# A two-layer mixer on one core: transfers of the divided sixth product moved from layer 1 to layer 0, and low parts used last

## The chip, the cores and the metric

One core of one Trainium2 chip. The metric is device time of one execution, in microseconds (us); runs of the same kernel differ by some tenths of a per cent. The work is matmuls in fp32 accuracy on TensorE (PE), with VectorE (DVE), ScalarE (ACT) and GpSimd (POOL) preparing operands, and two engines' queues issuing DMAs: SP (SyncE) and POOL.

## What is computed

The reference runs a linear-attention block and a gMLP block, twice, on x of 2048 x 512:

```python
def _A_ref(x, wqkv, wo):               # 32 heads of 16
    q, k, v = ...                      # x @ wqkv, split in heads
    pq, pk = phi(q), phi(k)            # phi(t) = (t + 1 if t > 0 else exp(t)) + 1e-6
    kv = einsum("bhsd,bhse->bhde", pk, v)
    z = einsum("bhsd->bhd", pk)
    o = (pq @ kv) / (pq . z + 1e-6)
    return o @ wo
def _B_ref(x, w_in, w_sp, b_sp, w_out):
    z = gelu(x @ w_in)                 # 2048 x 1792
    z1, z2 = z[..., :896], layernorm(z[..., 896:])
    g = w_sp @ z2 + b_sp               # w_sp is 2048 x 2048
    return (z1 * g) @ w_out
x = x + _A_ref(layernorm(x)); x = x + _B_ref(layernorm(x))   # layer 0
x = x + _A_ref(layernorm(x)); x = x + _B_ref(layernorm(x))   # layer 1, same weights
```

## The kernel before

**Stages.** Each layer (L = 0, 1) has four: P1 (class `P1`: K, Q, phi and the 512 x 512 product of k and v, a step s per 128 rows of x), P2 (the attention's output, then x @ w_in, gelu and layernorm, again by 128-row tiles, with a `tail` in layer 1), P4 (class `P4`: w_sp @ z2, the spatial mixing) and `out7` (the output stage, z1 * g times w_out, eight steps j, x added by accumulating DMA stores of POOL).

**Three matmuls for one.** Every fp32 operand is split in a high part (fp32r, made by ACT: L1678 for w_sp, L214 elsewhere) and a low part (operand less high part, made by DVE: L1681 for w_sp, L217 elsewhere). Each product runs as high x high, high x low, low x high (`mm3`, L228 to L230; for the spatial mixing `acc`, L1889 to L1891; in the output stage L2087 to L2089; in the tail L1145 to L1147).

**The spatial mixing.** w_sp @ z2 is cut into 2 x 2 blocks and done with seven block products instead of eight (a Strassen-Winograd scheme), in the order P2, P1, P6, P7, P4, P5, P3. A product is eight steps k, one per 128 rows of its block; in a step PE takes about 4.07 us. A product in `DIVIDED` (P2 and P4 in layer 0; P2, P4 and P5 in layer 1) is itself done by seven products of half the size, 7 x 2 steps (`SEVEN` gives their order; `mm_div`). The sixth product, P5, is so divided in layer 1 alone: this is the divided sixth product of the title.

**Sums of w_sp.** The products need sums of blocks of w_sp. Class `Sums` holds them in DRAM scratch, since both layers use the same w_sp: `s` and `s1` (made in layer 0's first half), `halves` (tile names hP: quarter sums that the divided products need) and `lows` (lowP). A hP tile of P4 or P5 is made in two transfers by `halve`: a *copy* from DRAM to DRAM on SP (L1551), 512 KB, and later an *add*, an accumulating DMA of POOL (L1555), 512 KB. `Sums.parts` lists them: 0 to 7 copies and 8 to 15 adds for P4, 16 to 23 copies and 24 to 31 adds for P5. `PARTS` says at which step of layer 0's mixing a part of P4 is issued; `P1.run` issues those of P5 in layer 1's steps s = 2 to 17 by `sums.halve(14 + s, None)`.

**Kept low parts.** `kept` names steps of P7 and P5 whose low part of w_sp layer 0 stores (SP, L1686) and layer 1 loads (POOL, L1684) in place of the subtraction L1681. With P5 divided in layer 1, six of its fourteen steps (k = 0, 1, 6, 7, 12, 13) take a kept one.

**What sets the order.** The schedule is written by hand: each engine executes in the order of the program, and so do SP's and POOL's DMA queues. `fetch1` (L1657, L1662) issues raw halves of w_sp on SP, `wsp` splits them two steps ahead of PE, `zsp` splits z (L1743 is the low part of z), `gate` (L1928 on DVE, L1930 on POOL) multiplies a finished unit of g by a page of z1, loaded on SP (L196, pg<-z). `wraw` loads pages of w_out on SP (L196, pg<-in_wout_dram). In layer 1's tail `wfetch` issues loads of sums of w_in on POOL (L205, pg<-w1s and pg<-w), and `e3` makes the layernorm's mean and variance of two z2 tiles with small column operations of POOL (L1074 in `e3m`; L1086 to L1088).

## Time and profile before

| what | value |
|---|---|
| median of 3 runs | 1353.8 us (1351.34 to 1356.03) |
| the profiled execution | 1351.78 us, its span 1350.0 us |
| TensorE clock granted | 1.00 |
| DMA | 294.50 MB, mean 218 GB/s |

In the profile a line of a group says the source line, the engine, the operation and `out<-in` by tile names: pg, qd and bg are pages (128 x 512), quads and larger tiles in SBUF, bank a PSUM bank, hP and lowP the scratch above. A row of a timeline is start, duration, engine, line, operation, and in brackets the idle time before it with what ended it. A row of windows gives the stretch, its length, busy time and number of instructions of PE, its weight loads, DVE, ACT and POOL, then the granted clock, the share of the sixteen DMA engines and GB/s. A row of DMA issues gives the size of one and the median us from issue to landing. A row of waits gives the total, the number and the longest.

From about 350 to 614 us runs the mixing of layer 0, to 692 its output stage, to 806 layer 1's P1, to 1016 its P2 with the tail, to 1272 its mixing (P7 from 1130, P5 from 1201) and to 1346 its output stage.

### The profile page before, as it was taken

The numbers are of one execution on the slowest core, as the hardware profiler recorded it, in microseconds if no ns is written. First come the engines' busy times: TensorE is split into PE (matmuls) and PEld (weight loads), VectorE is DVE, ScalarE is ACT, GpSimd is POOL, SyncE is SP. The second block draws the span as 40 slices with busy tenths as digits, with TensorE's granted clock in tenths as the row PEclk, the third lists the DMA queues.
The fourth block names the chain that finished last, engine by engine and source line by source line (L and its number), as shares of the span: only waits on it lengthen the run. The fifth ranks groups of instructions, "written<-read, shape, count | busy, mean of one in ns | idle before, by whom it ended". The sixth has DMA issues, their size and how long they took to land.

```text
span 1350.0 us, 19217 instructions
## 1 busy us (share of the span) xinstructions
PE 1340.0 (99%) x6540; PEld 1141.3 (85%) x6540; DVE 1037.7 (77%) x1658; ACT 726.3 (54%) x1219; POOL 463.8 (34%) x613
## 2 busy tenths in 40 slices
PE   9999999999999999999999999999999999999998
PEld 7888888888888888889988888888888888877898
DVE  7679877763797689897866877777689757889885
ACT  5774544334643255445667755556687333656454
POOL 3765765544122300301435453545450023022021
PEclk9999999999999999999999999999999999999999
DMA  5898477878877996843678783678767447479343
GB/s 183 277 311 281 164 264 252 289 262 263 296 241 266 299 292 208 291 164 64 152 192 287 208 199 94 204 249 252 235 195 252 143 171 264 155 242 315 106 78 64
DMA packets 174515, 294.50 MB, mean 218 GB/s; under 512 B 14544, under 2 KB 53968, under 8 KB 174160
## 3 DMA queue, kind: packets, MB, share of 16 engines
q1 hardware_dynamic: 155280, 253.67, 55.9%
q0 software_dynamic: 19136, 39.59, 13.4%
q8 instruction: 51, 0.84, 0.2%
q14 instruction: 48, 0.39, 0.1%
HBM read 206.18 MB, written 103.81 MB: 230 GB/s over the span
## 4 chain that ended last, share of the span: by engine, by line
PE 86%; DVE 4%; DMA 4%; issue 3%; ACT 1%; POOL 1%; SPq 0%; DVEq 0%; POOLq 0%; ACTq 0%
PE bank L1890 12%; PE bank L1891 12%; PE bank L1889 12%; PE bank L230 11%; PE bank L228 11%; PE bank L229 11%; PE bank L2087 3%; PE bank L2088 3%; PE bank L2089 3%; DMA qd<-lowP 1%; PE bank L988 1%; PE bank L987 1%; PE bank L986 1%; DMA pg<-xt 1%; PE bank L2101 1%
## 5 line engine op out<-in xcount | busy, mean ns | idle before, releaser
L1890 PE MATMUL bank<-qd,pg 128*128 128x512 f32 x760 | 296.1, 390 | 2.5 <-DMA qd<-lowP 1.7
L1889 PE MATMUL bank<-qd,pg 128*128 128x512 f32 x760 | 295.7, 389 | 0.0
L1891 PE MATMUL bank<-qd,pg 128*128 128x512 f32 x760 | 295.7, 389 | 0.0
L1678 ACT ACTIVATE qd<-qd 128x1024 fp32r<-128x1024 f32 x142 | 149.6, 1054 | 143.0 <-PE bank L1891 115.5
L1681 DVE TENSOR_TENSOR qd<-qd,qd 128x1024 fp32r<-128x1024 f32 x128 | 162.1, 1268 | 60.4 <-ACT qd L1678 60.4
L230 PE MATMUL bank<-qd,pg 128*128 128x512 f32 x448 | 174.8, 390 | 0.0
L1890 PEld LDWEIGHTS bank<-qd,pg 128*128 128x128 f32 x760 | 142.7, 188 | 33.3 <-DMA qd<-lowP 2.8
L1889 PEld LDWEIGHTS bank<-qd,pg 128*128 128x128 f32 x760 | 142.7, 188 | 29.7 <-ACT qd L1678 0.2
L1891 PEld LDWEIGHTS bank<-qd,pg 128*128 128x128 f32 x760 | 142.7, 188 | 29.5
L1930 POOL TENSOR_TENSOR bg<-bg,pg 128x512 f32<-128x512 f32 x28 | 47.9, 1710 | 213.6 <-DVE bg L1944 99.6
L228 PE MATMUL bank<-qd,pg 128*128 128x512 f32 x308 | 120.3, 391 | 0.3 <-DVE pg L217 0.3
L229 PE MATMUL bank<-qd,pg 128*128 128x512 f32 x308 | 120.0, 390 | 0.0
L230 PEld LDWEIGHTS bank<-qd,pg 128*128 128x128 f32 x448 | 84.1, 188 | 18.6 <-DVE pg L217 1.0
L363 POOL TENSOR_SCALAR rs<-mv 128x1 f32<-128x1 f32 x80 | 24.6, 308 | 197.4 <-DVE mv L361 188.0
L372 ACT ACTIVATE pg<-pg,nb,rs 128x512 f32<-128x512 f32 x52 | 42.1, 812 | 85.0 <-POOL nb L366 78.6
L1587 POOL TENSOR_TENSOR pg<-pg,pg 128x512 f32<-128x512 f32 x48 | 67.4, 1403 | 58.4 <-DMA pg<-in_wsp_dram 56.5
L214 ACT ACTIVATE pg<-pg 128x512 fp32r<-128x512 f32 x85 | 53.0, 624 | 63.1 <-DVE pg L448 18.2
L2089 PE MATMUL bank<-wo,qd 128*128 128x256 f32 x288 | 81.4, 283 | 0.0
L2087 PE MATMUL bank<-wo,qd 128*128 128x256 f32 x276 | 78.1, 283 | 0.0
L2088 PE MATMUL bank<-wo,qd 128*128 128x256 f32 x276 | 78.0, 283 | 0.0
L228 PEld LDWEIGHTS bank<-qd,pg 128*128 128x128 f32 x308 | 57.8, 188 | 12.6 <-DVE pg L217 0.7
L229 PEld LDWEIGHTS bank<-qd,pg 128*128 128x128 f32 x308 | 57.8, 188 | 12.1 <-DVE qd L217 0.3
(270 smaller groups left out, 3242.2 us busy)
## 6 DMA issues: line engine op xcount, KB each, us to landing
qd<-s SPq DMA_DIRECT2D x62, 512.0 KB, 4.3
qd<-in_wsp_dram SPq DMA_DIRECT2D x40, 512.0 KB, 4.0
qd<-hP SPq DMA_DIRECT2D x40, 512.0 KB, 4.6
pg<-z SPq DMA_DIRECT2D x56, 256.0 KB, 3.9
pg<-in_wsp_dram SPq DMA_DIRECT2D x52, 256.0 KB, 4.3
s<-pg SPq DMA_DIRECT2D x48, 256.0 KB, 3.7
z<-pg SPq DMA_DIRECT2D x40, 256.0 KB, 3.1
pg<-w POOLq DMA_DIRECT2D x38, 256.0 KB, 4.6
```

The source lines that it names most:

```text
L228: nc.tensor.matmul(out, ah, bh, start=start, stop=False)
L229: nc.tensor.matmul(out, ah, bl, start=False, stop=False)
L230: nc.tensor.matmul(out, al, bh, start=False, stop=stop)
L1587: nc.gpsimd.tensor_tensor(t, a, b, op=OP.add)
L1678: self.mark = nc.scalar.activation(w[:, 0], r, AF.Copy)
L1681: nc.vector.tensor_sub(w[:, 1], r, w[:, 0].bitcast(F32))
L1889: m(out, h[:, o], w[:, 0, j, :], start=start, stop=False, skip_group_check=True)
L1890: m(out, h[:, o], w[:, 1, j, :], start=False, stop=False, skip_group_check=True)
L1891: m(out, l[:, o], w[:, 0, j, :], start=False, stop=stop, skip_group_check=True)
L2087: m(out, A, x, start=start and f == 0, stop=False, skip_group_check=True)
L2088: m(out, A, y, start=False, stop=False, skip_group_check=True)
L2089: m(out, B, x, start=False, stop=stop and f == 2, skip_group_check=True)
```

## The change

1. The eight copies of P5 move from layer 1's P1 (s = 2 to 9) to the steps k = 0 to 7 of layer 0's P3, by `PARTS`.
2. The adds 24 to 27 move from layer 1's P1 (s = 10 to 13) to the first four steps of layer 0's output stage, after `join_b`. The adds 28 to 31 are issued as two halves each (256 KB), at s = 9 to 16 of layer 1's P1 (they were at s = 14 to 17).
3. `kept` leaves out the first four steps of P7: layer 0 makes four lowP stores less, layer 1 four lowP loads less and four subtractions more.
4. In layer 1, the kept steps of P5 use the low part of w_sp after the eight matmuls of a step that use its high part.
5. In layer 1's tail the column operations of the last tiles are issued behind the loads of `wfetch`: two `e3m` behind the first, and the three `e3r` operations of two tiles behind the second.

The lines of the changed kernel are some 8 to 31 higher: L1555 becomes L1572, L1551 L1565, L1681 L1698, L1686 L1703, L1728 to L1743 L1745 to L1760, L1086 to L1088 L1094 to L1096, L1074 L1075, L1657 and L1662 L1674 and L1679.

In layer 0's P3, SP issued these transfers before (qd<-s: raw halves; pg<-z: pages of z1; pg<-in_wout_dram: w_out):

```order
L196 DMA pg_571_5774<-z_0_0_5_2576 128x512
L1662 DMA qd_19_3764<-s_6_143 128x1024
L196 DMA pg_574_5817<-z_0_0_6_2692 128x512
L196 DMA pg_575_5819<-in_wout_dram 128x512
L196 DMA pg_576_5821<-in_wout_dram 128x512
L1662 DMA qd_19_3764<-s_7_144 128x1024
L196 DMA pg_579_5850<-z_0_1_4_3090 128x512
L196 DMA pg_584_5884<-z_0_1_5_3107 128x512
L196 DMA pg_587_5926<-z_0_1_6_3223 128x512
L196 DMA pg_588_5928<-in_wout_dram 128x512
```

and issues now, from the second copy on:

```order
L1565 DMA hP_1_1_168<-s_145 16x8192
L196 DMA pg_574_5815<-z_0_0_6_2692 128x512
L196 DMA pg_575_5817<-in_wout_dram 128x512
L196 DMA pg_576_5819<-in_wout_dram 128x512
L1679 DMA qd_19_3764<-s_7_144 128x1024
L1565 DMA hP_3_0_166<-s_145 16x8192
L196 DMA pg_579_5849<-z_0_1_4_3090 128x512
L1565 DMA hP_3_1_170<-s_145 16x8192
L196 DMA pg_584_5884<-z_0_1_5_3107 128x512
L1565 DMA hP_2_0_165<-s_145 16x8192
L196 DMA pg_587_5927<-z_0_1_6_3223 128x512
L196 DMA pg_588_5929<-in_wout_dram 128x512
```

Two copies stand ahead of the page z_0_1_4 and four ahead of the third w_out page; four more copies follow between later pages of z1.

In layer 1's tail, POOL had this order before (acc: the columns of mean and variance; w1s, w_3 and on: sums of w_in for PE):

```order
L1086 TENSOR_SCALAR acc<-acc 128x1
L1087 TENSOR_TENSOR acc<-acc,mhalf 128x1
L1088 TENSOR_SCALAR acc<-acc 128x1
...
L1074 TENSOR_SCALAR acc<-acc 128x1 x2
L205 DMA pg_981_10265<-w1s_1_0_119 128x512
L205 DMA pg_982_10267<-w1s_1_1_120 128x512
L205 DMA pg_984_10303<-w_3_0_101 128x256
```

and has now:

```order
L205 DMA pg_981_10257<-w1s_1_0_119 128x512
L205 DMA pg_982_10259<-w1s_1_1_120 128x512
L205 DMA pg_984_10295<-w_3_0_101 128x256
L205 DMA pg_985_10297<-w_3_1_102 128x256
L1075 TENSOR_SCALAR acc<-acc 128x1 x2
L205 DMA pg_986_10310<-w_4_0_103 128x256
L205 DMA pg_987_10312<-w_4_1_104 128x256
L1094 TENSOR_SCALAR acc<-acc 128x1
L1095 TENSOR_TENSOR acc<-acc,mhalf 128x1
L1096 TENSOR_SCALAR acc<-acc 128x1
```

The column operations (three each for two tiles) have gone behind the loads w1s, w_3 and w_4, ahead of w_5.

At the start of layer 1's P7, DVE had the evacuation of the product before (L1947) and then the z work of one step after another; before:

```order
L1947 TENSOR_TENSOR bg_26_10485<-bank_360_10816,pg_980_10250 128x512
L1728 TENSOR_TENSOR pg_1074_11325<-z_z_8642 128x384
L1730 TENSOR_TENSOR z_z_8642<-z_z_8642,z_z_9514 128x384
L1732 TENSOR_TENSOR z_z_9514<-z_z_8642,z_z_9514 128x384
L1733 TENSOR_TENSOR z_z_9514<-z_z_9514,z_z_8642 128x128
L1743 TENSOR_TENSOR pg_1076_11331<-pg_1074_11325,pg_1075_11330 128x384
L1728 TENSOR_TENSOR pg_1078_11341<-z_z_8739 128x384
```

and now:

```order
L1978 TENSOR_TENSOR bg_26_10485<-bank_360_10816,pg_980_10242 128x512
L1698 TENSOR_TENSOR qd_158_11322<-qd_126_10350,qd_158_11322 128x1024
L1745 TENSOR_TENSOR pg_1074_11325<-z_z_8642 128x384
L1747 TENSOR_TENSOR z_z_8642<-z_z_8642,z_z_9514 128x384
L1749 TENSOR_TENSOR z_z_9514<-z_z_8642,z_z_9514 128x384
L1750 TENSOR_TENSOR z_z_9514<-z_z_9514,z_z_8642 128x128
L1760 TENSOR_TENSOR pg_1076_11331<-pg_1074_11325,pg_1075_11330 128x384
L1698 TENSOR_TENSOR qd_159_11338<-qd_125_10220,qd_159_11338 128x1024
L1745 TENSOR_TENSOR pg_1078_11341<-z_z_8739 128x384
```

A subtraction of w_sp (qd) stands ahead of the z work (z_z, pg) of the second step and of the two behind it; the one of the first step stands ahead of the evacuation.

The diff:

```diff
@@ -111,7 +111,7 @@
 FILL = {7: 3, 9: 3, 11: 3, 13: 3, 15: 3}
 WADD = {2: 0, 4: 1, 6: 2}
 PARTS = {("P1", 4 + k): k for k in range(4)} | {("P6", k): 4 + k for k in range(8)}
-PARTS |= {("P7", k): 12 + k for k in range(4)}
+PARTS |= {("P7", k): 12 + k for k in range(4)} | {("P3", k): 16 + k for k in range(8)}
 LEFT = 4
 SPN = 3
 LOAD2 = (9, 10, 11, 14)
@@ -695,8 +695,8 @@
                     sums.add2(1, POOL2.get(s, 0))
                     sums.add2(0, DVE2.get(s, 0))
                 if self.L:
-                    if s > 1:
-                        sums.halve(14 + s, None)
+                    if 9 <= s < NT + 1:
+                        sums.halve(28 + (s - 9) // 2, None, (s - 9) % 2)
                     if s in WADD:
                         if not WADD[s]:
                             self.fsums = FSums()
@@ -1040,8 +1040,9 @@
             pages.put(self.S.pop(i)[0][1])
             while todo:
                 other()
-            self.e3m(i)
-            self.e3m(i + 1)
+            if i < NT - 2:
+                self.e3m(i)
+                self.e3m(i + 1)
 
         def e(self, i):
             n, k = divmod(i, 4)
@@ -1073,16 +1074,23 @@
                 a = self.zacc[i] if a is None else a
                 nc.gpsimd.tensor_scalar(a[:, 2:3], a[:, 0:1], a[:, 1:2], -1.0 / FH, op0=OP.add, op1=OP.mult)
 
-        def e3(self, i):
+        def e3(self, i, rest=True):
             if not self.L:
                 self.zms[i] = stats(ztile[i], 2)
                 return
-            a = self.zacc.pop(i)
+            a = self.zacc[i]
             self.e3m(i, a)
             nm, v, rs, nb = (a[:, k:k + 1] for k in range(2, 6))
             t = pages.get([P, FH], mybir.dt.bfloat16)
             nc.scalar.activation(t, ztile[i], AF.Square, bias=nm, accum_out=v)
             pages.put(t)
+            if rest:
+                self.e3r(i)
+
+        def e3r(self, i):
+
+            a = self.zacc.pop(i)
+            nm, v, rs, nb = (a[:, k:k + 1] for k in range(2, 6))
             nc.gpsimd.tensor_scalar(rs, v, 1.0 / FH, LN_EPS, op0=OP.mult, op1=OP.add)
             nc.gpsimd.tensor_tensor(rs, rs, mhalf, op=OP.pow)
             nc.gpsimd.tensor_scalar(nb, nm, rs, None, op0=OP.mult)
@@ -1231,6 +1239,12 @@
                 self.fmul(y, [t[:, 256:512] for t in ws[f]], self.T[6], False, False)
                 pages.put(*ws[f])
                 self.wfetch()
+                if f == 0:
+                    self.e3m(NT - 2)
+                    self.e3m(NT - 1)
+                if f == 1:
+                    self.e3r(NT - 4)
+                    self.e3r(NT - 3)
                 d.append(banks.whole(PAGE))
                 A(d[f], y, AF.Copy)
                 V.tensor_add(y, y, c[f])
@@ -1484,8 +1498,8 @@
                                 self.raw(1)
                                 quads.put(*self.xT.pop(2))
                                 self.T2()
-                                self.e3(NT - 4)
-                                self.e3(NT - 3)
+                                self.e3(NT - 4, False)
+                                self.e3(NT - 3, False)
 
                             self.epair(s - 4, late4, late3)
                         else:
@@ -1539,7 +1553,7 @@
                 at = ((j, k), (j, k + HT), (2 + j, k)) if h == 0 else ((2 + j, k + HT),)
                 self.raw.setdefault((k, j), []).extend(load(wsp_d[n, s], self.slots) for n, s in at)
 
-        def halve(self, n, after):
+        def halve(self, n, after, i=None):
 
             if not 0 <= n < len(self.parts):
                 return
@@ -1552,7 +1566,10 @@
             else:
                 if m in (2, 4):
                     src = self.halves[p, m // 2, q]
-                d = nc.gpsimd.dma_start(self.halves[p, m, q], src, accum_op=OP.add, max_dma_last_dim=4096)
+                dst = self.halves[p, m, q]
+                if i is not None:
+                    dst, src = dst[i:i + 1], src[i:i + 1]
+                d = nc.gpsimd.dma_start(dst, src, accum_op=OP.add, max_dma_last_dim=4096)
                 if after is not None:
                     behind(d, after)
 
@@ -1691,7 +1708,7 @@
 
         def kept(self, g):
             p, k = self.steps[g]
-            if p not in KEPT or p == "P3" and k > 4:
+            if p not in KEPT or p == "P7" and k < 4:
                 return None
             if p not in self.div:
                 t = self.sums.lows[p][:, k]
@@ -1806,8 +1823,22 @@
             name = "F" if r in (5, 3) else "X" if r in (1, 2) else "Y"
             if q == 0 and r in (1, 5):
                 self.bank[name] = [banks.get(PAGE) for _ in range(2)]
-            if q == 0 and r == 6:
-                pass
+            if self.L and self.kept(g) is not None:
+                M = nc.tensor.matmul
+                for x in range(2):
+                    for i in range(2):
+                        for f in range(2):
+                            o, b = slice(f * P, (f + 1) * P), self.bank[name][f]
+                            if x:
+                                M(b, h[:, i, o], w[:, 1, i, :], start=False, stop=r in (2, 4) and q == 1 and i == 1,
+                                  skip_group_check=True)
+                            else:
+                                M(b, h[:, i, o], w[:, 0, i, :], start=r == 1 and q == 0 and i == 0, stop=False,
+                                  skip_group_check=True)
+                                M(b, l[:, i, o], w[:, 0, i, :], start=False, stop=False, skip_group_check=True)
+                pages.put(h, l)
+                quads.put(w)
+                return
             for i in range(2):
                 for f in range(2):
                     self.acc(self.bank[name][f], h[:, i], l[:, i], slice(f * P, (f + 1) * P), w, i,
@@ -2179,6 +2210,8 @@
                     self.tick()
                 if nxt is not None:
                     self.join_b(j, nxt)
+                    if j < 4:
+                        self.sums.halve(24 + j, None)
                 self.omul(z, 3, y[:, lo], False, True)
                 if more or nxt is not None:
                     self.omul(z, 4, d[:, lo], False, True)
```

## The prediction

> **What bounds the kernel now.** I read three views in this order: the page's head and its chain of work that ended last, the waits of PE alone, and then a timeline around each of those waits.
>
> ```profile
> span 1350.0 us, 19217 instructions
> PE 1340.0 (99%) x6540; PEld 1141.3 (85%) x6540; DVE 1037.7 (77%) x1658; ACT 726.3 (54%) x1219; POOL 463.8 (34%) x613
> ...
> PE bank L617 <- DVE pg L612: 2.3, 1, 2.3
> PE bank L1890 <- DMA qd<-lowP: 1.7, 2, 0.9
> PE bank L1147 <- DMA pg<-w1s: 0.9, 1, 0.9
> PE bank L1890 <- DVE qd L1681: 0.8, 1, 0.8
> PE bank L228 <- DVE pg L217: 0.3, 1, 0.3
> ```
>
> The span is full of matmuls, and the number of matmuls doesn't change. So the change can only win what PE waits, and can only lose by making a new wait. The second list is all that PE waits for: the start (L617, 2.3 us), which the change doesn't touch, and five short waits, 1.7 + 0.9 + 0.8 + 0.3 = 3.7 us. The idle time counts from a matmul's modelled end, 0.39 us after its start, but matmuls follow each other every 0.227 us where nothing waits (1203.29 to 1203.52 below). So each stall is 0.16 us dearer than its row: 3.7 + 5 x 0.16 = **4.5 us**. That is the ceiling of the gain. The five are one each in layer 0's P4 product (506.73), layer 1's first half (755.78) and layer 1's tail (1006.60), and two in layer 1's P5 product.
>
> **Low parts last (P5 of layer 1).** Two lows loads (POOL, L1684) come too late:
>
> ```profile
> 1197.02 0.72 POOL L1684 DMA_DIRECT2D qd<-lowP  x1 [3.18 <-DMA qd<-hP]
> ...
> qd<-lowP POOLq DMA_DIRECT2D x1, 512.0 KB, 7.8
> ...
> 1203.29 0.39 PE L1891 MATMUL bank<-qd,pg 128*128 128x512 f32 x1
> 1203.52 0.39 PE L1889 MATMUL bank<-qd,pg 128*128 128x512 f32 x1
> 1204.82 0.50 PE L1890 MATMUL bank<-qd,pg 128*128 128x512 f32 x1 [0.91 <-DMA qd<-lowP]
> ...
> 1229.75 0.72 POOL L1684 DMA_DIRECT2D qd<-lowP  x1 [1.96 <-PE bank L1891]
> ...
> qd<-lowP POOLq DMA_DIRECT2D x1, 512.0 KB, 8.9
> ...
> 1237.45 0.39 PE L1889 MATMUL bank<-qd,pg 128*128 128x512 f32 x1
> 1238.66 0.50 PE L1890 MATMUL bank<-qd,pg 128*128 128x512 f32 x1 [0.83 <-DMA qd<-lowP]
> ```
>
> The first load lands at 1197.02 + 7.8 = 1204.8, the second at 1229.75 + 8.9 = 1238.65. Both are wanted by the second matmul of a step. The change puts eight matmuls ahead of the first low one, so the low part is wanted 8 x 0.227 = 1.8 us after the step's start: at 1205.3 and 1239.3, which leaves 0.5 and 0.6 us. The same matmuls run, in another order. The issue of the second load follows PE (its releaser is L1891), so an earlier PE moves issue and need together. Gain: (1204.82 - 1203.52 - 0.23) + (1238.66 - 1237.45 - 0.23) = **2.05 us**.
>
> **The tail of layer 1's second half.** POOL issues the w1s loads behind small column operations:
>
> ```profile
> 992.97 0.73 POOL L1086 TENSOR_SCALAR acc<-acc 128x1 f32<-128x1 f32 x1 [2.78 <-ACT pg L1084]
> ...
> 1000.15 1.18 POOL L205 DMA_DIRECT2D pg<-w1s  x2
> ...
> 1005.35 0.39 PE L1146 MATMUL bank<-bg,pg 128*128 128x512 f32 x1
> 1006.60 0.50 PE L1147 MATMUL bank<-bg,pg 128*128 128x512 f32 x1 [0.86 <-DMA pg<-w1s]
> ```
>
> The six L1086 to L1088 instructions and two L1074 ones, which fill POOL from 992.97 to 1000.15, now stand behind these loads. The loads still need the page that the second Square of ACT (L1084) frees, early in this stretch, so they go out some 6 of these 7.2 us earlier, against a lateness of 1006.60 - 1005.35 - 0.23 = **1.0 us**. The price is that two w_5 loads go out behind the column chain; I cost it at nothing, since the chain (about 6 us of POOL) now runs beside matmuls that already have their weights. If that cover is short, the loss is at most the 1.0 us won.
>
> **Four kept lows less in layer 0.** The P4 stall is the end of a chain that starts with SP's queue:
>
> ```profile
> 466.00:500.00 34.00, 34.00 (x152) 28.15 (x151) 28.10 (x51) 15.05 (x22) 3.26 (x4) 1.00 1.03 312
> ...
> lowP<-qd SPq DMA_DIRECT2D x6, 512.0 KB, 11.1
> ...
> 497.37 1.06 ACT L1678 ACTIVATE qd<-qd 128x1024 fp32r<-128x1024 f32 x1 [0.92 <-DMA qd<-hP]
> ...
> 505.45 1.23 DVE L1681 TENSOR_TENSOR qd<-qd,qd 128x1024 fp32r<-128x1024 f32 x1 [0.26 <-ACT qd L1678]
> ...
> 505.53 0.44 PE L1889 MATMUL bank<-qd,pg 128*128 128x512 f32 x1
> 506.73 0.50 PE L1890 MATMUL bank<-qd,pg 128*128 128x512 f32 x1 [0.76 <-DVE qd L1681]
> ```
>
> The sixteen DMA engines are full from 466 to 500 (share 1.03), ACT waits for raw halves, and DVE, whose order is fixed, is late with its subtraction. At the window's 312 GB/s a 512 KB transfer takes about 1.7 us, so the three stores that fall into it less free about 5 us of queue. The chain is about 1 us late. Gain: 506.73 - 505.53 - 0.23 = **1.0 us**. It is an indirect gain, and the first to fail: if what sets DVE's time is its own order and not the loads, nothing is won.
>
> In layer 1 four DVE subtractions, of 1.23 us each like that at 505.45, take the place of the loads:
>
> ```profile
> 1126.00:1138.00 12.00, 12.00 (x54) 9.95 (x53) 11.02 (x22) 4.43 (x6) 2.19 (x3) 1.00 0.63 201
> ...
> 1132.62 0.55 DVE L1743 TENSOR_TENSOR pg<-pg,pg 128x384 fp32r<-128x384 f32 x1
> ...
> 1134.61 0.39 PE L1891 MATMUL bank<-qd,pg 128*128 128x512 f32 x1
> ```
>
> One falls into the idle time before this window; three go into a DVE that is 11.02 of 12 us busy. The second step's low part of z is ready at 1132.62 + 0.55 = 1133.2 and used at 1134.61; 1.2 us more leaves 0.2 to 0.3. The next two steps gain more room on PE (4.07 us a step) than they lose. Bounds: 0, and 4 x 1.2 = 4.8 us, if nothing hides them. I take 0.1, near the first row's room.
>
> **Copies out of layer 1's first half, halved adds.** The stall there follows a transpose that waited for xt behind copies on SP:
>
> ```profile
> 700.00:760.00 60.00, 59.75 (x263) 49.12 (x263) 42.54 (x76) 40.84 (x73) 29.35 (x44) 1.00 0.83 275
> ...
> 742.40 0.73 DVE L448 STREAM_TRANSPOSE bank<-pg 128x512 f32<-128x512 f32 x1 [1.17 <-DMA pg<-xt]
> ...
> 755.78 0.50 PE L228 MATMUL bank<-qd,pg 128*128 128x512 f32 x1 [0.25 <-DVE pg L217]
> ```
>
> Eight copies leave this stretch, and four of the eight adds after it; the other four are cut in two. The xt loads behind the copies land earlier. Gain: 0.25 + 0.16 = **0.4 us**; bound below, nothing.
>
> **What the moved transfers cost in layer 0.** SP now issues eight 512 KB copies among the last loads of the P3 product:
>
> ```profile
> 583.00:614.00 31.00, 31.00 (x143) 25.85 (x142) 28.10 (x47) 12.57 (x20) 0.00 (x0) 1.00 0.40 136
> ...
> 588.11 4.71 SPq L196 DMA_DIRECT2D pg<-z  x3
> 592.93 0.37 SPq L196 DMA_DIRECT2D pg<-in_wout_dram  x1
> ...
> pg<-z SPq DMA_DIRECT2D x1, 256.0 KB, 4.6
> ...
> 593.98 0.68 DVE L1928 TENSOR_TENSOR bg<-bg,pg 128x512 f32<-128x512 f32 x1
> ...
> 608.35 1.76 DVE L217 TENSOR_TENSOR qd<-bg,qd 128x1536 fp32r<-128x1536 f32 x1 [1.55 <-ACT qd L214]
> ...
> 614.05 0.28 PE L2089 MATMUL bank<-wo,qd 128*128 128x256 f32 x1
> ...
> qd<-in_wsp_dram SPq DMA_DIRECT2D x1, 512.0 KB, 15.2
> ```
>
> There is room in bytes: eight copies move 4.2 MB in and 4.2 MB out, while the stretch is 0.40 full. But the z and wout loads queue behind them, at about 2 us a copy (an estimate: 4.2 MB at 275 GB/s, the rate of the stretch that holds the copies now, is 15 us). Two copies stand ahead of the z page that DVE adds at 593.98, four ahead of the wout load of 592.93. Behind 593.98 on DVE stand the subtractions that feed PE and the chain to the low part at 608.35, ready at 608.35 + 1.76 = 610.1 and wanted by PE at 614.05: 3.9 us of room, and DVE has 31.0 - 28.1 = 2.9 us idle in between to catch up. The z page lands now at 588.11 + 4.6 = 592.7, 1.3 us ahead of its use; two copies make it 2 to 4 us later, so DVE waits 0.7 to 2.7 us for it, less than its idle time. The wout load has four copies ahead of it and a longer lead (its use by DVE is behind 593.98 too). Bounds: 0, and 6.1 us (the slower rival below, from the 15.2 us row). I take **0.2 us**: the nearest row is the 2.9 us of idle time, which covers nearly all of it.
>
> In the output stage, POOL issues three of the four adds behind x stores; the first goes out in P3 already, as POOL is idle there (x0). I cost them at nothing: PE waits for none of POOL's work between 614 and 692, by the list of waits.
>
> By the Trainium skill ("DMA: Bandwidth & Descriptors", section "Queues, rings and completion order") each DMA engine takes turns between queues, a packet at a time, so the one add in P3 shares the engines with SP's loads rather than waiting for them. The trace agrees that lows loads of POOL and SP's loads slow each other (8.9 us for 512 KB at 1229.75); by that rule the z page of 593.98 would be one more 512 KB transfer late, 1.7 us at the rate of the full stretch, so DVE 2.4 to 4.4 us late against 2.9 us of idle time, and the sum up to 1.5 us less.
>
> **The sum.** 2.05 + 1.0 + 1.0 + 0.4 = 4.45 us won, 0.1 + 0.2 = 0.3 us given back: -4.15 us. The profiled execution took 1351.8 us (1.8 around its span of 1350.0), so it becomes 1347.6. The three runs of before and that one have a mean of 1353.2, 1.5 above it; so I expect **1349.1 us** of the changed kernel, 0.31% less.
>
> **The rivals.**
> *A, only the stalls attacked head-on go.* The P5 pair and the tail give 3.05 us. The P4 and first-half stalls stay, because DVE's own order sets them. For it: at 505.45 DVE waits 0.26 us for ACT, not for a DMA, and between 466 and 500 it is busy 28.1 of 34 us. Against it: ACT waits 0.92 us for a load just before. 1353.2 - 3.05 + 0.3 = 1350.5 us, inside 0.3%.
> *B, a new wait in layer 1 gives part back.* The four subtractions find no room: the second step's low is late by 1 us, and each of the next three by as much again until DVE catches up, 1 to 3 us. For it: DVE 11.02 of 12. Against: the 5 us that DVE waits for PE just before. 1350 to 1352 us.
> *C, slower.* The mechanism: SP's copies starve the loads of P3. Price: the z page issued at about 588.5 takes 14.5 us, as loads did when the engines were full (lows stores 11.1, the raw load 15.2); it lands at 603 instead of being used at 593.98. DVE is 9.0 us late, has 2.9 to catch up, and PE waits 6.1 us at the start of the output stage. 1349.1 + 5.9 = 1355.0 us. It decides from a lateness of 2.9 us on DVE, and eats the whole gain at 7.3. Against it: the same copies in the stretch from 700 to 760 left it 0.83 full, with 275 GB/s.
> *D, the reordering doesn't help.* The lows load is 0.5 us later than here, since its issue moves with what precedes it; then a stall of under 0.5 us each stays. It gives about 1350 us.
>
> **How the numbers follow.** Forecast 0.50, A 0.18, B and D together 0.18, C 0.14. About 0.3% (4.06 us) is what a measurement of this kernel can tell from no change. The forecast lies just past it; four fifths of its chance and a tenth of the others' count as faster: 0.45. Slower by over 0.3% needs C with a second load as late: 0.11. The rest, 0.44, is within. The range goes from 1345 (no give-back, and the lower of the runs, 1351.3 - 4.45 = 1346.9, and below it by the 2.0 us that the profiled execution lies under the median of before, 1353.8) to 1355.5, C's price with half a microsecond.
>
> **What would show it.** The list of PE's waits should have lost its last four rows: no L1890 (now L1921) wait on lows, none at the tail for w1s. If A holds, a wait on L1681 (now L1698) is still there near 506. If B holds, a new one stands near 1130 on L1743 (now L1760). If C holds, PE waits near 614 for DVE L217, or in P3 from 600 on, and DVE's wait for a z page shows at about 594. The prediction is wrong if PE's waits sum to more than 3.5 us.

## The result, and the profile after

The changed kernel takes **1346.34 us** (median of 6 runs, 1345.65 to 1346.85) against 1353.24 us of the kernel before (6 runs, 1351.34 to 1356.03): a ratio of **0.9949**, with a 95% interval of 0.9936 to 0.9962. Measured again on other runs it was 1346.72 us (1346.41 to 1348.54) against 1352.47, ratio 0.9955 (0.9941 to 0.9969). The prediction said 1349.1 us: the direction and the mechanism were right, the gain is 6.9 us (5.8 in the second series) where 4.15 were forecast. The runs also lie closer together, 1.2 us apart in the first series where those of before lie 4.7 apart.

The page of the changed kernel's profile begins so:

```profile
span 1343.9 us, 19206 instructions
PE 1337.6 (100%) x6540; PEld 1141.7 (85%) x6540; DVE 1043.3 (78%) x1662; ACT 727.0 (54%) x1219; POOL 462.8 (34%) x613
```

and these are all of PE's waits that it lists:

```profile
PE bank L617 <- DVE pg L612: 2.3, 1, 2.3
PE bank L228 <- ACT pg L214: 0.2, 1, 0.2
```

The same 6540 matmuls, 6.1 us less span: the four lines that the prediction wanted gone are gone, and only the wait of the start and one of 0.2 us are left. DVE has become busier by 5.6 us (four subtractions, 1662 instructions for 1658) and nothing waits for it.

The stretches that the prediction worked with, in the changed kernel (length, busy time of PE, weight loads, DVE, ACT, POOL, then clock, DMA share, GB/s):

```profile
583.00:614.00 31.00, 31.00 (x149) 26.10 (x148) 27.55 (x45) 13.80 (x22) 0.00 (x0) 1.00 0.67 254
466.00:500.00 34.00, 34.00 (x151) 28.15 (x150) 31.59 (x58) 18.50 (x29) 3.25 (x4) 1.00 0.92 279
700.00:760.00 60.00, 60.00 (x266) 49.67 (x266) 45.95 (x81) 43.53 (x77) 31.45 (x47) 1.00 0.70 220
1126.00:1138.00 12.00, 12.00 (x55) 9.94 (x54) 11.89 (x22) 4.43 (x6) 1.51 (x2) 1.00 0.54 175
```

The load has moved as the edits say: layer 0's P3 from 136 to 254 GB/s, layer 1's first half from 275 to 220, the full stretch from 466 to 500 from 312 to 279. In that last one DVE got through 58 instructions instead of 51, for the raw halves came earlier: from 466 to 506 us ACT waits for one of them once, where it waited four times before, 4.4 us in all. In P7 of layer 1 DVE is now busy 11.89 us of 12, which is where a new wait would have stood. ACT's one wait for a raw half:

```profile
490.66 1.06 ACT L1695 ACTIVATE qd<-qd 128x1024 fp32r<-128x1024 f32 x1 [0.97 <-DMA qd<-in_wsp_dram]
```

How near the new waits came, in three places. The second lows load of P5's last kept steps (POOL, then its DMA, then PE):

```profile
1226.26 0.72 POOL L1701 DMA_DIRECT2D qd<-lowP  x1 [2.68 <-issue]
...
qd<-lowP POOLq DMA_DIRECT2D x1, 512.0 KB, 7.9
...
1231.80 1.07 PE L1833 MATMUL bank<-qd,pg 128*128 128x512 f32 x4
...
1234.30 0.39 PE L1838 MATMUL bank<-qd,pg 128*128 128x512 f32 x1
1234.52 0.84 PE L1833 MATMUL bank<-qd,pg 128*128 128x512 f32 x3
```

It lands at 1226.26 + 7.9 = 1234.2, and L1833 uses a low part first at 1234.52: 0.3 to 0.4 us of room. Used second, it would have been wanted seven matmuls, 1.6 us, earlier. In P7 and at the end of P3, DVE and PE:

```profile
1130.31 0.55 DVE L1760 TENSOR_TENSOR pg<-pg,pg 128x384 fp32r<-128x384 f32 x1
...
1131.16 0.39 PE L1922 MATMUL bank<-qd,pg 128*128 128x512 f32 x1
...
593.45 0.69 DVE L1959 TENSOR_TENSOR bg<-bg,pg 128x512 f32<-128x512 f32 x1 [0.23 <-DMA pg<-z]
...
607.84 1.76 DVE L217 TENSOR_TENSOR qd<-bg,qd 128x1536 fp32r<-128x1536 f32 x1 [1.56 <-ACT qd L214]
...
612.66 0.28 PE L2120 MATMUL bank<-wo,qd 128*128 128x256 f32 x1
```

In P7 the second step's low part is ready at 1130.86, 0.30 us ahead of its use; the prediction had 0.2 to 0.3. In P3, DVE waits 0.23 us for the z page that two copies were put ahead of, and the last low part is ready at 609.6, 3.1 us ahead of its use where it was 3.9. So the copies took 0.8 us of that room and no time.

### The profile page after: what moved, and what is told of

Its sections match the earlier page's. It is cut to its first block, busy times and chain, and to the rows that moved or that the text cites. A ratio compares the mean times of both kernels' runs of the same rounds, so it can differ in the third digit from the quotient of the medians.

```text
span 1343.9 us, 19206 instructions
## 1 busy us (share of the span) xinstructions
PE 1337.6 (100%) x6540; PEld 1141.7 (85%) x6540; DVE 1043.3 (78%) x1662; ACT 727.0 (54%) x1219; POOL 462.8 (34%) x613
## 4 chain that ended last, share of the span: by engine, by line
PE 99%; DVE 0%; ACT 0%; issue 0%; DVEq 0%
PE bank L230 14%; PE bank L229 14%; PE bank L228 14%; PE bank L1922 12%; PE bank L1920 12%; PE bank L1921 12%; PE bank L2118 3%; PE bank L2119 3%; PE bank L2120 3%; PE bank L986 1%; PE bank L987 1%; PE bank L988 1%; PE bank L384 1%; PE bank L1153 1%; PE bank L1155 1%; PE bank L1154 1%
## 5 line engine op out<-in xcount | busy, mean ns | idle before, releaser
L1920 PE MATMUL bank<-qd,pg 128*128 128x512 f32 x736 | 286.3, 389 | 0.0
L1921 PE MATMUL bank<-qd,pg 128*128 128x512 f32 x736 | 286.3, 389 | 0.0
L1922 PE MATMUL bank<-qd,pg 128*128 128x512 f32 x736 | 286.3, 389 | 0.0
L1698 DVE TENSOR_TENSOR qd<-qd,qd 128x1024 fp32r<-128x1024 f32 x132 | 167.8, 1273 | 53.2 <-ACT qd L1695 53.2
L230 PE MATMUL bank<-qd,pg 128*128 128x512 f32 x448 | 174.7, 390 | 0.0
L1921 PEld LDWEIGHTS bank<-qd,pg 128*128 128x128 f32 x736 | 138.1, 188 | 28.8
L1922 PEld LDWEIGHTS bank<-qd,pg 128*128 128x128 f32 x736 | 138.1, 188 | 28.7
L1920 PEld LDWEIGHTS bank<-qd,pg 128*128 128x128 f32 x736 | 138.1, 188 | 28.5
L228 PE MATMUL bank<-qd,pg 128*128 128x512 f32 x308 | 120.2, 390 | 0.2 <-ACT pg L214 0.2
L229 PE MATMUL bank<-qd,pg 128*128 128x512 f32 x308 | 120.0, 390 | 0.0
L230 PEld LDWEIGHTS bank<-qd,pg 128*128 128x128 f32 x448 | 84.0, 188 | 18.1 <-DVE pg L217 0.4
L228 PEld LDWEIGHTS bank<-qd,pg 128*128 128x128 f32 x308 | 57.8, 188 | 12.3 <-ACT pg L214 0.4
L229 PEld LDWEIGHTS bank<-qd,pg 128*128 128x128 f32 x308 | 57.8, 188 | 12.1 <-DVE qd L217 0.3
```

The source lines that it names most:

```text
L228: nc.tensor.matmul(out, ah, bh, start=start, stop=False)
L229: nc.tensor.matmul(out, ah, bl, start=False, stop=False)
L230: nc.tensor.matmul(out, al, bh, start=False, stop=stop)
L1698: nc.vector.tensor_sub(w[:, 1], r, w[:, 0].bitcast(F32))
L1920: m(out, h[:, o], w[:, 0, j, :], start=start, stop=False, skip_group_check=True)
L1921: m(out, h[:, o], w[:, 1, j, :], start=False, stop=False, skip_group_check=True)
```

## The experiments

The theory going in: each stall has one cause among the edits, undoing an edit brings its stalls back, and the sizes add up. The rival: the gain comes from lighter DMA traffic, the edits depend on each other, and a stall is no fixed thing. All times are medians; each series has its own runs of the kernel before, so ratios stand beside.

### One part undone at a time

Low parts used second again:

```diff
-            if self.L and self.kept(g) is not None:
-                M = nc.tensor.matmul
...
+            if q == 0 and r == 6:
+                pass
```

> The changed kernel with layer 1's kept P5 steps back in the old order (low part of w_sp used by the second matmul). Theory 1, each stall has its own cause and the gains add up: the two stalls in P5 come back, 1.07 + 0.99 us late in the profile of before, and each costs another 0.11 us, since the matmul behind a stall takes 0.34 instead of 0.23 us to the next: 2.3 us, so about 1348.6 us. PE's waits show two on lowP of 0.8 to 0.9 us. Theory 2, the gain comes from lighter DMA traffic and the parts depend on each other: with the copies and half the lows of P7 gone the lows of P5 land in time without the reordering, and nothing or less than 1 us comes back, 1346.3 to 1347.3.

Measured: 1348.82 us, ratio 0.9977 (0.9967 to 0.9986), so 2.5 us of the gain are gone. Two waits are back, the longer one:

```profile
1202.25 0.50 PE L1907 MATMUL bank<-qd,pg 128*128 128x512 f32 x1 [1.27 <-DMA qd<-lowP]
1202.59 0.39 PE L1908 MATMUL bank<-qd,pg 128*128 128x512 f32 x1
```

The first theory's number, within 0.2 us. Lighter traffic alone doesn't do it: with all other edits in, PE waits 1.27 and 0.83 us for these loads, where it waited 0.91 and 0.83 before.

The tail's order as before:

```diff
...
-                if f == 0:
-                    self.e3m(NT - 2)
-                    self.e3m(NT - 1)
-                if f == 1:
-                    self.e3r(NT - 4)
-                    self.e3r(NT - 3)
...
-                                self.e3(NT - 4, False)
-                                self.e3(NT - 3, False)
+                                self.e3(NT - 4)
+                                self.e3(NT - 3)
```

> The changed kernel with layer 1's tail as before (the column operations on POOL ahead of the w1s loads). Theory 1: one stall of 1.0 us and 0.11 behind it comes back at the matmul that uses w1s, about 1347.5 us. Theory 2: the w1s loads, 7.3 us from issue to landing in the changed kernel, now come in lighter traffic and land in time; nothing comes back.

Measured: 1347.66 us, ratio 0.9966 (0.9953 to 0.9978), 1.3 us of the gain gone; the wait for w1s is back, and a wait of 0.2 us on lowP stands in P5:

```profile
PE bank L1147 <- DMA pg<-w1s: 1.0, 1, 1.0
PE bank L1819 <- DMA qd<-lowP: 0.2, 1, 0.2
```

The first theory again.

All steps of P7 kept again:

```diff
-            if p not in KEPT or p == "P7" and k < 4:
+            if p not in KEPT or p == "P3" and k > 4:
```

> The changed kernel with the first four steps of P7 kept again (four stores more in layer 0, four loads more and four subtractions less in layer 1). Theory 1: the stall of 1.0 us in layer 0's P4 product comes back, with 0.11 behind it, about 1347.5 us, and DVE's subtractions there stand 4 us later again. Rival A of the prediction (DVE's own order sets this stall, not SP's queue): nothing comes back there, 1346.3. Nothing else of the change acts ahead of this place, so theory 2 says the same as theory 1 here, unless the lows of P5 are late again in layer 1: then up to 1 us more.

Measured: 1348.87 us (1347.12 to 1351.27), ratio 0.9974 (0.9964 to 0.9984): 2.5 us gone, where 1.1 were expected. The stall near 507 is back at its size:

```profile
PE bank L1921 <- DVE qd L1698: 0.8, 1, 0.8
```

So rival A is out: the four stores set this stall, not DVE's own order. (They load both SP's queue and the DMA engines; the runs don't part the two.) But it is not all. The edit also does a thing that neither theory had. POOL issues the second lows load of P5, the first of the prediction's two late ones, later when eight lows of P7 were loaded before it; in this run

```profile
1195.73 0.72 POOL L1701 DMA_DIRECT2D qd<-lowP  x1 [3.23 <-DMA qd<-hP]
```

and in the run with this edit alone (below)

```profile
1196.18 0.71 POOL L1684 DMA_DIRECT2D qd<-lowP  x1 [1.99 <-PE bank L1891]
```

The idle time ahead of it is 3.2 us in all six profiles that keep eight lows of P7, with another releaser, and 2.0 in all six that keep four (the two of the ladder and the bunched copies, below, not counted). So fewer lows in P7 also bring P5's second load 1.2 us forward. They put P5's last load back by as much: from its issue to the matmul that would use it second lie 7.9 us in those six profiles with eight lows and 6.7 in the six with four, and for the second load it is the other way about.

How much of the 2.5 us that explains can be counted. PE executes the same number of matmuls in the same order in this run as in the changed kernel, so their starts can be compared one by one. This profile is 2.7 us longer than that of the changed kernel: 1.2 us at the stall near 507, 0.3 in P5 (its low parts, though used last, are late), 0.25 behind the last matmul (4.31 us to the end of the span in place of 4.06; all profiles with eight lows have 4.3, all with four 4.05 or 4.06), and 0.8 ahead of 350 us, where none of the edits acts.

Copies and adds of P5 back in layer 1's first half:

```diff
-PARTS |= {("P7", k): 12 + k for k in range(4)} | {("P3", k): 16 + k for k in range(8)}
+PARTS |= {("P7", k): 12 + k for k in range(4)}
...
-                    if 9 <= s < NT + 1:
-                        sums.halve(28 + (s - 9) // 2, None, (s - 9) % 2)
+                    if s > 1:
+                        sums.halve(14 + s, None)
...
-                    if j < 4:
-                        self.sums.halve(24 + j, None)
```

> The changed kernel with the copies of P5 back in layer 1's first half, and the eight whole adds there. Theory 1: the stalls at 755.8 and 775.6 come back, 0.41 + 0.14 us and 0.11 behind each, about 0.8 us: 1347.1 us. Theory 2: DMA in the first half of layer 1 decides more than the profile of one execution shows (the median of before lies 1.5 us over its profiled execution, that of the changed kernel 0.7): 1.5 us or more comes back, and the runs spread by 2 us or more, as those of before do (1351.3 to 1356.0).

Measured: 1347.10 us (1346.27 to 1349.45), ratio 0.9966 (0.9953 to 0.9978): 0.8 us gone, as expected, but the trace doesn't show the expected place. No stall stands at 755 or 775; this one does, near 1024:

```profile
PE bank L1918 <- DVE qd L1695: 0.2, 1, 0.2
```

The size agrees with the first theory, the profile doesn't, and the runs spread by 3.2 us, as the second said. By the starts of the matmuls nothing is lost in layer 1's first half here: 0.6 us of this profile's 1.2 lies ahead of 350 us and 0.6 near 1024. The four losses add up to 7.1 us, against a gain of 6.9. (By the ratios, against the 0.9955 of the second series of the changed kernel, they are 3.0, 1.5, 2.6 and 1.5 us, each uncertain by some 2.4 by the two intervals; those of the tail and of the copies are not clear of that.)

### Is a stall the same in every execution?

The kernel before, unchanged, profiled a second time:

> The kernel before, unchanged, profiled a second time, to see which of its stalls are the same in every execution. Theory 1: the same five, at the same places within 0.3 us of size. Theory 2 (some of them are a matter of the execution): the waits on DMAs and on the subtraction near 506 differ by more than 0.5 us, or the waits in layer 1's first half (755.8, 775.6) are absent, as they are in the run with the copies back in that place.

```profile
PE bank L617 <- DVE pg L612: 2.3, 1, 2.3
PE bank L1890 <- DMA qd<-lowP: 1.8, 3, 1.1
PE bank L1147 <- DMA pg<-w1s: 1.0, 1, 1.0
PE bank L1890 <- DVE qd L1681: 0.6, 1, 0.6
PE bank L228 <- ACT pg L214: 0.2, 1, 0.2
```

Four are there again, within 0.3 us; the waits for the lows are three now (1.06, 0.19 and 0.53 us), and that of layer 1's first half (L217) is missing. So P5, the tail and P4 are constant in kind, and the stall at 755 is a matter of the execution. Its absence in the run above then says little. Of the five profiles with the copies in layer 1's first half, three have one interval between matmuls there that is 0.15 us or more too long (0.41, 0.27, 0.18); of the nine without them none has. By the starts of the matmuls that half costs 0.85 to 0.89 us in these three, 0.17 and 0.00 in the other two, and 0.00 in all nine. As far as these profiles go, the copies make that loss possible.

The run with all of P7 kept, again:

> The changed kernel with P7's first four steps kept again, profiled a second time: its twelve runs spread from 1347.1 to 1351.3 us, those of the changed kernel from 1345.7 to 1346.9. If the full DMA stretch before layer 0's P4 product sets the spread, the stall near 507 has another size than 1.03 us here, or a second stall stands beside it; if the spread comes from elsewhere, it is 1.0 us again and another place differs.

1347.08 us in this execution. The stall near 507 was 1.03 us again, and a second one of 0.42 us stood a microsecond ahead of it, for ACT's high part: the place is the same, its size is not. What the slow ones of its runs (up to 1351.3) do more isn't shown by either profile.

### One part alone

The moved copies and adds alone, on the kernel before (the diff above, the other way round):

> The kernel before with the moved copies and the moved and halved adds alone. Theory 1: the stalls at 755.8 and 775.6 go, 0.8 us less than before (1351.5), the other four stay. Theory 2: the copies cause no stall by themselves in the first half, and the time stays within 0.4 us of before. Either way no new wait of PE from 600 to 620.

Measured: 1351.87 us against 1352.55, ratio 0.9993 (0.9984 to 1.0003): inconclusive in time. There is no wait from 600 to 620, and none in the first half. But this profile, of an execution of 1353.16 us, holds what the others lacked. PE in P5:

```profile
1204.60 0.50 PE L1893 MATMUL bank<-qd,pg 128*128 128x512 f32 x1 [1.84 <-DMA qd<-lowP]
...
1206.05 0.63 PE L1892 MATMUL bank<-qd,pg 128*128 128x512 f32 x1
1206.48 0.63 PE L1893 MATMUL bank<-qd,pg 128*128 128x512 f32 x1
```

and by stretches, the clock in the third column from the end:

```profile
1202.22:1205.63 3.41, 1.57 (x7) 0.98 (x6) 3.41 (x6) 0.63 (x1) 0.60 (x1) 1.00 0.94 294
1205.63:1209.04 3.41, 3.41 (x10) 2.64 (x8) 0.82 (x2) 0.77 (x2) 0.00 (x0) 0.50 0.44 167
1209.04:1212.45 3.41, 3.41 (x16) 2.82 (x15) 2.02 (x3) 3.41 (x7) 0.51 (x1) 1.00 0.03 5
```

The lows load came 1.84 us after PE was ready for it, and a microsecond after PE went on the granted clock fell to half for 3.41 us: matmuls follow each other every 0.43 us instead of 0.227, which with the restart (the matmul behind a stall starts 0.11 us late) costs another 1.8 us. A wait of 1.8 us costs 3.8.

Fewer lows alone (`p == "P7" and k < 4` in `kept`):

> The kernel before with the first four steps of P7 no longer kept, alone. Theory 1 by the profile: the stall near 506 goes, 1.1 us less (1351.2). By the leave-one-out run, which lost 2.5 us: 2.5 us less (1349.8), and a spread of runs under 4 us. The P5, tail and first-half stalls stay.

Measured: 1350.33 us, ratio 0.9981 (0.9973 to 0.9990), 2.2 us less (2.6 by the ratio). The stall near 506 is gone, and so is the first of P5's, which was expected to stay; 0.5 us of the second is left. Spread 2.9 us. The earlier issue found above fits the first: its load has 7.9 us here and takes 7.6. But it isn't enough by itself. In the run without low parts last the load has the same 7.9 us and takes 9.3, and PE waits; the two loads, this run's first:

```profile
qd<-lowP POOLq DMA_DIRECT2D x1, 512.0 KB, 7.6
...
qd<-lowP POOLq DMA_DIRECT2D x1, 512.0 KB, 9.3
```

Low parts last alone (the hunk of `mm_div`):

> The kernel before with the low parts used last in P5 alone. By the stalls of the two profiles of before, 2.3 to 2.6 us less than before (1350.1 of 1352.5). If some executions of before wait longer than 1.8 us for these loads and pay a slow clock too, as the run with the moved copies did, the median gains more than 2.6 us and the runs above 1353 are gone.

Measured: 1349.89 us against 1351.72, ratio 0.9982 (0.9973 to 0.9991), 1.8 us less (2.4 by the ratio). No wait for lows is left in its profile. The highest of its eleven runs is 1351.25, where five of the fifteen of before lie above 1353. That fits the theory with the slow clock in part. Of those five, two (1353.27 and 1353.98 us) ran at a mean granted clock of 1.000, and a slow stretch as long as the one above takes 0.0013 off it; so slow clocks aren't what all of them have in common. The median also gained less than the theory says.

### What a longer wait costs

The subtraction L1698 repeated on DVE at five places of the changed kernel:

```diff
+AGAIN = {(0, "P1", 6): (8, 1), (0, "P6", 5): (9, 1), (1, "P1", 5): (13, 0), (1, "P6", 5): (10, 0), (1, "P3", 4): (7, 0)}
...
                 nc.vector.tensor_sub(w[:, 1], r, w[:, 0].bitcast(F32))
+                full, half = AGAIN.get((self.L, *self.steps[g]), (0, 0))
+                for _ in range(full):
+                    nc.vector.tensor_sub(w[:, 1], r, w[:, 0].bitcast(F32))
+                for _ in range(half):
+                    nc.vector.tensor_sub(w[:, 1, 0], r[:, 0], w[:, 0, 0].bitcast(F32))
```

> The changed kernel, with the subtraction L1698 repeated on DVE at five places far apart in the mixing (the result of a repetition is what stands there already), so that PE waits there for DVE: by the slack of each place in the profile of the changed kernel, about 1.4 us in layer 0's P1 product, 1.1 in its P6, 2.2 in layer 1's P1, 1.6 in its P6 and 3.0 in its P3. In the run with the moved copies alone, a wait that made PE 2.0 us late was followed by matmuls at a granted clock of 0.54 for 3.2 us, which cost 1.8 us more; waits up to 1.43 us late, in all runs so far, cost 0.11 us more and no slow clock. Theory 1, there is a length of wait beyond which the clock drops: the long ones (2.2, 3.0) show it, the short ones (1.1, 1.4) don't, and the total is 9.3 us of waits + 0.5 + two times 1.8 = about 1359.7. Theory 2, the slow stretch came from something else at that place: no slow clock, about 1356.

Measured: 1377.56 us, with waits far longer than worked out (2.1 in two parts, 4.9, 3.4 in two parts, 4.5 and 3.0 us): the expected short ones never came about. All five were followed by a slow clock. The first, in which PE waited twice:

```profile
422.85 0.50 PE L1927 MATMUL bank<-qd,pg 128*128 128x512 f32 x1 [0.93 <-DVE qd L1704]
424.51 0.50 PE L1928 MATMUL bank<-qd,pg 128*128 128x512 f32 x1 [1.16 <-DVE pg L1766]
```

and the stretches behind it and behind the second one:

```profile
424.60:429.20 4.60, 4.60 (x14) 3.64 (x15) 4.57 (x7) 0.00 (x0) 0.00 (x0) 0.63 0.95 345
...
462.40:466.80 4.40, 4.39 (x11) 3.40 (x12) 4.40 (x6) 0.00 (x0) 0.12 (x1) 0.54 0.70 233
466.80:470.00 3.20, 3.20 (x16) 2.60 (x15) 3.08 (x5) 1.59 (x2) 3.20 (x3) 1.00 0.87 269
```

So the slow clock of the run before was not an accident of that place. Two waits of 0.93 and 1.16 us within two microseconds are enough; one of 1.27 us (the run without low parts last) is not, and one of 1.84 us is.

The clock's own records in the traces show what decides. In every profile, once PE has reached the full clock, the clock changes only at the ends of stretches of 3.41 us that run on whatever the program does: 1334.6, 1338.0 and 1341.4 us at full clock in the undisturbed profiles are 391, 392 and 393 of them, and each slow time in the program is one, two or three of them, at 0.50. The last wait of this run, 2.96 us, falls into two such stretches, and the wait of 1.27 us of the run without low parts last into one (this run's rows first):

```profile
1275.38:1278.80 3.42, 2.09 (x10) 1.39 (x8) 3.35 (x3) 0.00 (x0) 0.00 (x0) 1.00 0.01 2
1278.80:1282.21 3.41, 1.78 (x7) 1.26 (x8) 3.38 (x7) 0.00 (x0) 0.00 (x0) 1.00 0.00 0
1282.21:1285.62 3.41, 3.41 (x10) 2.64 (x9) 3.38 (x7) 3.08 (x6) 0.00 (x0) 0.50 0.21 77
...
1199.40:1202.81 3.41, 2.14 (x9) 1.44 (x9) 3.41 (x5) 1.11 (x2) 1.41 (x1) 1.00 0.88 252
1202.81:1206.22 3.41, 3.41 (x16) 2.82 (x15) 1.86 (x4) 1.72 (x3) 0.00 (x0) 1.00 0.72 239
```

PE is idle for 1.33 us in the first stretch, and the next runs at full clock; it is idle for 1.63 us in the second, and the next runs at half. In all fourteen profiles, up to the last matmul, the seven full-clock stretches with 1.63 us or more of idle PE are each followed by a slow one, and none with 1.33 us or less is. So idle time adds up within a stretch, and where a wait falls counts as much as its length.

The Trainium skill ("TensorE: Matmul & The Clock Gate", section "Part 1: The HAM clock gate (the "warmup" mystery)") has the clock at half after one idle window of some 3.4 us, windows that run free of the program. The 0.43 us between matmuls agrees with its half rate, and the 3.41 us with its window. The idle time needed doesn't agree: here 1.63 us within a window did it, under half of one, and the measurement decides.

### All copies at once

Eight copies in P3's third step instead of one per step:

```diff
-PARTS |= {("P7", k): 12 + k for k in range(4)} | {("P3", k): 16 + k for k in range(8)}
+PARTS |= {("P7", k): 12 + k for k in range(4)}
...
                     self.sums.halve(PARTS.get((p, k), -1), self.mark)
+                    for n in range(16, 24) if (p, k) == ("P3", 2) else ():
+                        self.sums.halve(n, self.mark)
```

> The changed kernel with all eight copies of P5 issued together in the third step of P3 (k = 2), ahead of the z page that DVE adds near 593.4, in place of one per step. At about 1.65 us a copy the page lands near 605, DVE is 12 us late and has 2.9 us of idle time to catch up. Rival C of the prediction as a mechanism: PE waits 5 to 7 us in all from 603 on, 1351 to 1355 us with what the clock does. If the room in P3 is larger than it was worked out to be (the z pages are not what PE waits for), under 1348 us.

Measured: 1359.78 us, ratio 1.0047 (1.0031 to 1.0064). On DVE:

```profile
609.03 0.69 DVE L1959 TENSOR_TENSOR bg<-bg,pg 128x512 f32<-128x512 f32 x1 [15.24 <-DMA pg<-z]
```

PE waits 8.4 us for the subtraction behind it, then runs the next 4.7 us at half clock:

```profile
PE bank L1921 <- DVE qd L1698: 8.4, 1, 8.4
...
613.10:617.80 4.70, 4.68 (x12) 3.62 (x13) 4.70 (x8) 1.21 (x3) 0.00 (x0) 0.53 0.19 45
```

The same eight copies, in the same product, cost nothing one per step and about 13 us at once. That is outside the 1351 to 1355 us expected: the page was issued at 594.55, behind the copies, and took 14.5 us, so it landed at 609 and not 605, and the clock came on top. The mechanism of rival C is real and dearer than its 6.1 us; the spacing keeps the change out of it.

### The changed kernel again

> The changed kernel once more, unchanged, against new runs of the kernel before. The four runs with one part undone lost 2.5, 1.3, 2.5 and 0.8 us against the changed kernel's 1346.34, 7.1 in all, while the stalls that left the profile add up to 5.9. If the rest is that some executions of before pay a slow clock behind a stall (or other waits that the one profile didn't hold), the ratio is 0.995 again, the runs stay within 1.5 us, and no wait of PE over 0.4 us is in the profile besides the start. If the first measurement was lucky, the ratio is 0.9956 or more, the 5.9 us of the profile, and the spread is as wide as that of before.

Measured: 1346.72 us, ratio 0.9955 (0.9941 to 0.9969), between the two, and runs 2.1 us apart, so neither expectation holds whole. Its profile is of the slowest run (1348.54) and shows two waits beside the start:

```profile
PE bank L1921 <- DVE qd L1698: 0.7, 1, 0.7
PE bank L1833 <- DMA qd<-lowP: 0.3, 1, 0.3
```

The first stands at 1025.6, where one was with the copies undone too: ACT waited 1.98 us for a page whose store to z had not landed (1.58 with the copies undone, 0.66 in the first profile):

```profile
1024.20 0.72 ACT L1803 ACTIVATE pg<-z_z 128x256 fp32r<-128x256 f32 x2 [1.98 <-DMA z<-pg]
```

The second is P5's last kept step: the low part used last was still late by 0.5 us, for its load, the one that the third edit issues 1.2 us later, took 8.7 us here (7.9 in the first profile). Another 1.3 us of this execution are lost ahead of 350 us. By the starts of the matmuls that stretch, in which no edit acts, differs by 1.9 us among the fourteen profiles, as much as a part is worth, so two profiles can't price a part by their lengths alone. The room of 0.3 to 0.4 us read above is thinner than the difference from one execution to another.

## Why the prediction came out as it did

**What bounds the kernel: right.** PE's waits were nearly the whole of what the change won (0.25 of 6.1 us stand behind the last matmul), and all four rows went.

**The ceiling of 4.5 us: wrong, and here the sum failed.** The step is "each stall is 0.16 us dearer than its row". It is 0.27: behind a stall the next matmul also starts 0.11 us late (1202.25 to 1202.59 above is 0.34, not 0.23; behind each of the five stalls of before it is the same). For five stalls that is 0.55 us. The list of waits also left out two losses under its resolution, at 775.6 (0.25 us with the restart) and at 196.9 (0.3, ahead of everything the change touches). With these, 5.6 of the 6.1 us between the two profiled executions are found, and 5.85 with the 0.25 behind the last matmul; the rest is in intervals too small to single out. The measured time lies inside the stated range all the same, but the range's lower end was set by the spread of the runs, not by dearer stalls: that much was luck.

**One execution stood for all.** The remaining 0.8 us, up to the medians' 6.9, are not in the two profiles, and in the second series, with 5.8 us between the medians, nothing remains. The kernel before has runs up to 1356; a wait for the lows of 1.84 us turned into 3.8 through the clock in an execution of 1353.16, and runs above 1353 vanish with the low parts used last alone. The clock doesn't make up all of this spread. Of some seventy runs of the kernel before whose granted clock is on record, seven lie above 1355 us, and four of these have 0.998, which no other has; but ten of the fifteen between 1353 and 1355 have 1.000. What those pay for isn't shown: no profile of a run above 1354 was taken.

**Low parts last, 2.05 us:** 2.5 undone, 1.8 alone. Right in mechanism.

**The tail, 1.0 us:** 1.3 undone. Right, and undersized by the restart. No price for the late w_5 loads was seen.

**Fewer kept lows, 1.0 us:** 2.5 undone, 2.2 alone. The indirect chain from the four stores was right, and rival A, which gave it nothing, is refuted. Mis-sized: with the restart the stall is 1.0 to 1.6 us in the six profiles that have it, and 0.25 us stands behind the last matmul; no place was found for the rest. The edit also moves two lows loads of P5, one 1.2 us forward and one as much back, where the prediction put all of P5 on the other edit. That is no sure gain: PE loses 0 to 0.3 us in P5 in the three profiles with eight lows of P7 and low parts last, and 0 to 0.7 in the six with four; with low parts second it loses 2.4 to 5.0 in three profiles with eight, and 0.9 and 2.7 in the two with four. Whether the two edits overlap in P5 stays open: if both removed the same stall, each would be worth more alone than undone, and the medians have it the other way, within their uncertainty.

**Copies out of the first half, 0.4 us:** 0.8 undone, 0.7 alone, neither clear of noise. The profiles give the sign: up to 0.89 us lost there with the copies, nothing without them. The stall that was quoted is absent in other profiles of the same kernel, so one wait of 0.3 us was too thin a row to rest a term on.

**What is given back, 0.3 us:** nothing measurable. The four subtractions were hidden with 0.3 us to spare, the copies with 3.1. Rival B didn't come about; rival D did in one execution of the second series, for 0.5 us, through the load that the fewer kept lows put back.

**Rival C:** refuted for this change and confirmed as a mechanism by the bunched copies. Its price left out the clock, and that the page itself is issued some 6 us later behind the copies.

## What to carry to other kernels

On a kernel that is 99% PE, read PE's waits one by one and price each from start to start, restart included; then ask of each how it varies, with a second profile, before resting a term on it. A wait near a microsecond is cheap to leave and dear to let grow: in this case, once PE idled for about half of one of the clock's 3.41 us stretches, a wait of 1.84 us cost double. A transfer that must move goes into a stretch with room one piece per step: the same bytes at once starved the loads behind them.

## What was not expected of the hardware

The clock of PE falls after far less idleness than a long pause: 1.63 us of idle PE or more within one 3.41 us stretch gave, behind the wait, 3.4 to 5.4 us at a granted clock of 0.50, at a price of 1.7 to 2.7 us each, restart included; 1.33 us or less gave none. The threshold was not narrowed further. The longest wait in the two profiles of the kernel before, behind the start, is 1.06 us.
